# Attention's ScalarE and VectorE work issued behind the latest tanh and multiplication, in a fused attention and two-layer feed-forward kernel on one core

## The chip, the cores and the metric

The kernel runs on one core of a Trainium2 chip. The metric is device time in microseconds (us) of one execution. A core has TensorE (PE in the profile, with weight loads as PEld), VectorE (DVE), ScalarE (ACT), GpSimd (POOL) and SyncE (SP, which here issues nearly all DMAs). Each engine works through its own instructions in the order in which they stand; semaphores make one engine wait for another.

## The reference

Three parts follow each other, all in float32. Attention has 4 batches of 8 heads, 576 positions and 64 channels; it is computed twice, once on means of four neighbouring positions (144 x 144 scores) and once locally, in a band of 7 positions, and the two outputs are added. The result, 2304 tokens by 512 channels, goes through two feed-forward layers with 2048 hidden channels.

```python
out_up = np.repeat(sm_attn(q_d, k_d, v_d), factor, axis=2)      # q_d, k_d, v_d: means of 4 positions
scores = np.where(np.abs(pos[:, None] - pos[None, :]) < factor, scale * q @ k.T, -1e9)
x = out_up + softmax(scores) @ v                                 # (2304, 512) after a transpose
h = x @ w_in;  x = (h * (1 / (1 + np.exp(-1.702 * h)))) @ w_out  # layer 1
h = x @ w_in2; out = np.where(h > 0, h, np.exp(np.minimum(h, 0)) - 1) @ w_out2   # layer 2
```

## The kernel before

Every float32 operand of the layers is split into a high and a low part that TensorE multiplies at full rate (type float32r); a product is the sum of three of four partial products (high x high, high x low, low x high). ScalarE makes the high part by a copy, VectorE the low part by a subtraction.

**Units of attention.** `Unit(b, hp, ...)` is one batch and one pair of heads. Its work is cut into pieces (`pieces`, L608): `trans` or `turn` (turns q and k; batches 2 and 3 do it on VectorE), `qk` (local scores, tiles `qk`, then `sl` and row maxima `nm` on VectorE), `qk_down` (scores of the means, `qkd`, `nmd`), `exps` (exponentials on ScalarE into `sl` and `pd`, with their sums), `weigh` (division by the sums on VectorE), `pdt` and `pt` (transposes on TensorE into PSUM tiles `pdt` and `ptr`, copied to `pdT` and `PT`), `pv_down` and `pv` (products with v; the result goes to the layer's input `x32`, "x" in the rows). The PSUM tiles of all pieces share a pool `spool` of two buffers (tag `s`) once the first phase is over. A list `queue` holds the pieces of all units in order; `attend()` (L718) takes the next one, and one deferred group of three exponentials.

**Layer 1.** Tokens are in blocks (`BLOCKS1`: 256, 256, 512, 512, 512, 256). A step is one block and one inner tile (two tiles of 128 hidden channels for a block of 256 tokens, one for 512): `products_h1` (L746) multiplies x by w_in into PSUM tile `h` (two buffers), then ScalarE's tanh writes `g` (L767), VectorE multiplies (L770), ScalarE copies the high part `g1h` (L771) and VectorE subtracts the low part `g1l` (L772). `products_y1` (L780) multiplies these by w_out two steps later (`LAG`) into `y`; after the last tile of a block, `ye` goes to DRAM (`ydram`). `ye` and `g` share the two buffers of tag `g`. Steps 0 to 15 are those of blocks 0 and 1, in alternation from step 4 on (step 12 is tile 4 of block 1, step 15 its tile 7); steps 16 to 31 are block 2, 32 to 47 block 3, 48 to 63 block 4, 64 to 71 block 5.

**What sets the order.** The loop at L985 walks the steps. A step's products are generators that yield between parts, and at each yield the loop calls `attend()` once (L1016). Before a block's first step, `split_some` splits its x into `xh` and `xl` (L299, L300). A planner then orders each engine's instructions by priority and modelled readiness and keeps dependences; `tc.issue_after(ins)` adds the order (no wait) that what is traced inside the block stands behind `ins` on the engine of `ins`. It is used in layer 2 already, in `behind` (L257).

Of the kernel before, what the change touches and what calls it, by code (L numbers as in the profile page):

```python
# [15 lines left out]
AF = mybir.ActivationFunctionType  # L16
ALU = mybir.AluOpType
# [10 lines left out]
NK = 4  # L28
# [28 lines left out]

NEXTRA = 6
AHEAD = 3


def win_start(w):
# [4 lines left out]
def kernel(  # L67
# [20 lines left out]
    nc = tc.nc  # L88
# [18 lines left out]
    for half in range(2):  # L107
        rows = slice(64 * half, 64 * half + 64)
        for a, e, lo in ((0, 1, -3), (1, 5, 0), (5, 6, 3)):
            m = mask[rows, a:e, :]  # L110
            for step, base, mult in ((1, -lo, -1), (-1, lo + 6, 1)):
                nc.gpsimd.affine_select(
                    out=m, in_=m, pattern=[[0, e - a], [step, KW]], compare_op=ALU.is_ge, fill=NEG,
# [133 lines left out]
    def w_in(layer, f, c, part):  # L247
        return wts[layer, "i", f][:, part, c, :]
# [7 lines left out]
    @contextmanager  # L256
    def behind():  # L257
        with ExitStack() as stack:
            for ins in urgent.values():
                stack.enter_context(tc.issue_after(ins.ins))  # L260
            yield
# [24 lines left out]
    def block_of(gw):  # L286

        return next(i for i, (t0, n) in enumerate(BLOCKS1) if t0 <= 64 * gw < t0 + n)

    def split_x(blk, c):  # L290
        if blk not in xsplit:

            n = BLOCKS1[blk][1]
            nb = 2 if blk == 0 else 1
            parts = [xpool.tile([P, nb, NK, n], F32R, tag=f"x{p}", name=f"x{p}_{blk}") for p in "hl"]
            for i in range(nb):
                xsplit[blk + i] = [t[:, i] for t in parts]
        hi, lo = xsplit[blk]
        nc.scalar.activation(out=hi[:, c, :], in_=x32[blk][:, c, :], func=AF.Copy)  # L299
        nc.vector.tensor_tensor(  # L300
            out=lo[:, c, :], in0=x32[blk][:, c, :], in1=hi[:, c, :].bitcast(F32), op=ALU.subtract
        )
# [385 lines left out]
    for i, u in enumerate(units + [None]):  # L688
        front, nback = pieces[u] if u is not None else ([], [])
# [25 lines left out]
    def ready(blk):  # L715
        return not due[blk]

    def attend():  # L718

        if deferred:  # L720
            deferred.pop(0)()
        if not queue:
            return False
        piece, ends = queue[0]
        if ends is not None and block_of(ends.b * NWIN + ends.w1 - 1) >= nsplit[0] // NK + XBUFS:
            return False
        queue.pop(0)
        piece()
        if ends is not None:
            for users in due.values():  # L730
                users.discard(ends)
        return True

    def split_some(blk):

        if blk < NBLK and nsplit[0] < NK * (blk + 1) and ready(blk):
            split_x(blk, nsplit[0] % NK)
            nsplit[0] += 1

    hg = {}  # L740

    def tiles_of(blk):

        return 512 // BLOCKS1[blk][1]

    def products_h1(blk, st):  # L746

        xh, xl = xsplit[blk]
        nf, tb = tiles_of(blk), BLOCKS1[blk][1]
        ph = hpool.tile([P, nf, tb], F32, tag="h", name=f"h1_{blk}_{st}")  # L750
        done = 0
        for i in range(nf):
            f = nf * st + i
            n = 0
            for wp, xp in ((0, xh), (0, xl), (1, xh)):
                for c in range(NK):
                    nc.tensor.matmul(  # L757
                        out=ph[:, i, :], lhsT=w_in(1, f, c, wp), rhs=xp[:, c, :],
                        start=(n == 0), stop=(n == 3 * NK - 1),
                    )  # L760
                    n += 1
                    done += 1
                    if done == 6 * nf:
                        yield
        g = gpool.tile([P, nf, tb], F32, tag="g", name=f"g1_{blk}_{st}", bufs=2)

        nc.scalar.activation(out=g, in_=ph, func=AF.Tanh, scale=0.851)  # L767
        gh = gpool.tile([P, nf, tb], F32R, tag="gh", name=f"g1h_{blk}_{st}")
        gl = gpool.tile([P, nf, tb], F32R, tag="gl", name=f"g1l_{blk}_{st}")
        nc.vector.scalar_tensor_tensor(out=g, in0=g, scalar=1.0, in1=ph, op0=ALU.add, op1=ALU.mult)  # L770
        ins = nc.scalar.activation(out=gh, in_=g, func=AF.Copy)  # L771
        copied = nc.vector.tensor_tensor(out=gl, in0=g, in1=gh.bitcast(F32), op=ALU.subtract)  # L772
        if blk == NBLK - 1:
            urgent.update(act=ins, dve=copied)
        hg[blk, st] = (gh, gl)
        yield
# [106 lines left out]
    def split_y(bi, c):  # L883
        t0, n = blocks[bi]
        if bi not in x2:
            pool = x2pools[bi % 2]
            x2[bi] = [pool.tile([P, NK, 512], F32R, tag=f"x2{p}", name=f"x2{p}_{bi}") for p in "hl"]
        hi, lo = x2[bi]
        t = y32.pop((bi, c))
        nc.scalar.activation(out=hi[:, c, :n], in_=t[:, :n], func=AF.Copy)  # L890
        nc.vector.tensor_tensor(  # L891
            out=lo[:, c, :n], in0=t[:, :n], in1=hi[:, c, :n].bitcast(F32), op=ALU.subtract
        )
# [32 lines left out]
    def hidden2(s):  # L926
# [3 lines left out]
        if bi + 1 < len(blocks):  # L930
            if 8 <= f < 8 + NK:
                load_y(bi + 1, f - 8)
            if 10 <= f < 10 + NK:
                split_y(bi + 1, f - 10)
        wt2.load(AHEAD + wt2.half - wt2.loaded)
        with behind():
# [42 lines left out]
    def rate(si):  # L979
        if due[1] and si < 8:  # L980
            return RATE0
        return RATE1

    waiting, prev = [], None
    for si, (blk, f2) in enumerate(steps + [(None, None)] * LAG):  # L985
        chunks = []
        if blk is not None:
            while not ready(blk):
                assert attend()
            if blk > 1 and f2 == 0:  # L990

                for _ in range(NK):
                    split_some(blk)
                while waiting:
                    prev = waiting.pop(0)
                    wt1.need("o", tiles_of(prev[0]) * (prev[1] + 1) - 1)
                    chunks.append(products_y1(*prev))
            while nsplit[0] < NK * (blk + 1):
                split_some(blk)
            wt1.need("i", tiles_of(blk) * (f2 + 1) - 1)  # L1000
            chunks.append(products_h1(blk, f2))
            waiting.append((blk, f2))
            if blk == NBLK - 1:
                used |= {f"wi{2 * f2}", f"wi{2 * f2 + 1}"}
        if len(waiting) > LAG or blk is None:
            prev = waiting.pop(0)
            wt1.need("o", tiles_of(prev[0]) * (prev[1] + 1) - 1)
            chunks.append(products_y1(*prev))
        if blk is None:
            hidden2(si - len(steps))  # L1010
        nchunk = 0
        for chunk in chunks:
            for _ in chunk:
                if not wt1.finished() and blk == 0:
                    wt1.convert()
                for _ in range(rate(si)):  # L1016
                    attend()
                if blk == 0:
                    split_some(1)
                nchunk += 1  # L1020
                if wt2 is not None and nchunk in (2, 3) and (nchunk == 2 or si % 2):
                    wt2.load(AHEAD + wt2.half - wt2.loaded)
                    with behind():
                        wt2.convert()
        if blk == NBLK - 1:
            if 1 <= f2 <= NK:
                load_y(0, f2 - 1)
            if 3 <= f2 < 3 + NK:
                split_y(0, f2 - 3)
        if chunks and prev is not None and prev[0] == NBLK - 1:  # L1030
            used |= {f"wo{2 * prev[1]}", f"wo{2 * prev[1] + 1}"}
        if wt1.finished() and stage1 is not None:
            ls1.close()
            stage1 = None
        if not queue and nsplit[0] == NK * NBLK and l1a is not None:
            l1a.close()
            l1x.close()
            l1s.close()
            hpools.append(ls2.enter_context(tc.tile_pool(name="hpool2", bufs=2, space=PSUM, side="right")))
            l1a = None  # L1040
            stage2 = ls2.enter_context(tc.tile_pool(name="stage2", bufs=1, side="right"))
            x2pools.append(ls2.enter_context(tc.tile_pool(name="x2a", bufs=1, side="right")))
            wextra = ls2.enter_context(tc.tile_pool(name="wextra", bufs=1, side="right"))
            for i, tile2 in enumerate(order2):
                places[(2, *tile2)] = (wextra, f"we{i}") if i < NEXTRA else (wpool, released[i - NEXTRA])
            used |= {f"we{i}" for i in range(NEXTRA)}
            wt2 = Weights(2, order2, stage2, 3, lambda tag: tag in used, 0)
            wt2.load(AHEAD)
    assert not queue
# [46 lines left out]
```

## Time and profile before

| | |
|---|---|
| runs of the kernel before, us | 991.32, 990.57, 985.33 (median 990.57) |
| profiled execution, its own time, us | 992.29 |
| its span from first to last instruction, us | 990.5 |
| mean granted TensorE clock | 0.983 |
| TensorE busy, share of the span | 97% |
| VectorE and ScalarE busy | 50% and 47% |

A busy time counts the instructions that run, also when they run slowly: TensorE's granted clock stands beside it, in shares of full speed. Two levels occur, 2.4 GHz (1.0) and 1.2 GHz (0.5). In the rows an instruction's end is modelled, so that pipelined instructions overlap: the pace of a run of matmuls is read from one start to the next. A wait is written as [idle before <- what ended it].

### The profile page before, as it was taken

To read this page: it belongs to the slowest core of one execution; us is meant where nothing else is said; L and a number is where in the kernel's file an instruction comes from. 1 tells how busy PE (TensorE), PEld (TensorE's weight loads), DVE (VectorE), ACT (ScalarE), POOL (GpSimd) and SP (SyncE) were. 2 spreads that over 40 slices of the span, in tenths; PEclk is the share of its full clock that TensorE was granted. 3 is DMA by queue.
4 is the path that set the end of the run, shared out by engine and by line. 5 is a ranking of instruction groups with operands and counts; after the bars stand their busy time and mean duration, and the time that the engine had idled before them with its cause. 6 is when DMAs were issued, how large, how long until landed. Compare 5 with 4: busy or idle time off the path is not lost. (4 is left out here: it accounts for less than half of the span.)

```text
span 990.5 us, 15177 instructions
## 1 busy us (share of the span) xinstructions
PE 957.7 (97%) x6028; PEld 789.3 (80%) x6028; DVE 499.6 (50%) x898; ACT 468.5 (47%) x1116; POOL 69.9 (7%) x117
## 2 busy tenths in 40 slices
PE   7988999998999999999999989999999999999998
PEld 4557888976777877888888987877888888888897
DVE  2888898655555453232223898785223222322232
ACT  4899976444344362223224565665334333433343
POOL 4330034112011010000000000000000000000000
PEclk9989999988999999999999999999999999999999
DMA  9756823423222010301004960002001100100010
GB/s 188 218 159 179 251 50 55 90 44 77 50 51 61 25 52 16 126 1 43 1 1 135 357 219 11 1 1 86 1 0 32 43 1 1 54 0 1 1 43 22
DMA packets 113846, 68.01 MB, mean 69 GB/s; under 512 B 80752, under 2 KB 103792, under 8 KB 113776
## 3 DMA queue, kind: packets, MB, share of 16 engines
q1 hardware_dynamic: 109040, 65.87, 23.5%
q10 hardware_dynamic: 4736, 1.18, 0.7%
q8 instruction: 47, 0.77, 0.3%
q14 instruction: 23, 0.19, 0.1%
HBM read 57.59 MB, written 9.44 MB: 68 GB/s over the span
## 5 line engine op out<-in xcount | busy, mean ns | idle before, releaser
L792 PE MATMUL y<-g1h,whl1o 128*128 128x256 f32 (+1 forms) x768 | 208.5, 344 | 0.0
L954 PE MATMUL o<-whl2o,g2h 128*128 128x512 f32 x576 | 181.4, 395 | 3.7 <-ACT ye L801 3.4
L757 PE MATMUL h<-xh,whl1i 128*128 128x256 f32 (+1 forms) x768 | 171.5, 346 | 3.7 <-ACT xh L299 2.7
L905 PE MATMUL h<-x2h,whl2i 128*128 128x512 f32 (+1 forms) x640 | 158.9, 370 | 0.0
L792 PEld LDWEIGHTS y<-g1h,whl1o 128*128 128x128 f32 x768 | 135.8, 191 | 17.2 <-issue 1.0
L757 PEld LDWEIGHTS h<-xh,whl1i 128*128 128x128 f32 x768 | 124.2, 191 | 22.3 <-ACT xh L299 3.5
L915 DVE SCALAR_TENSOR_TENSOR g<-e,h 128x512 f32<-128x512 f32 (+1 forms) x80 | 50.7, 633 | 180.0 <-ACT e L913 179.8
L905 PEld LDWEIGHTS h<-x2h,whl2i 128*128 128x128 f32 x640 | 114.3, 188 | 22.5
L954 PEld LDWEIGHTS o<-whl2o,g2h 128*128 128x128 f32 x576 | 107.5, 189 | 28.6 <-ACT ye L801 3.8
L792 PE MATMUL y<-g1l,whl1o 128*128 128x256 f32 (+1 forms) x384 | 129.9, 339 | 0.0
L912 ACT ACTIVATE e<-h 128x512 f32<-128x512 f32 (+1 forms) x80 | 44.3, 554 | 161.6 <-PE h L905 161.6
L954 PE MATMUL o<-whl2o,g2l 128*128 128x512 f32 x288 | 113.1, 393 | 0.0
L770 DVE SCALAR_TENSOR_TENSOR g<-g,h 128x512 f32<-128x512 f32 x72 | 49.2, 684 | 121.2 <-ACT g L767 121.2
L767 ACT ACTIVATE g<-h 128x512 f32<-128x512 f32 x72 | 42.8, 595 | 134.2 <-PE h L757 128.0
L757 PE MATMUL h<-xl,whl1i 128*128 128x256 f32 (+1 forms) x384 | 88.1, 344 | 0.0
L905 PE MATMUL h<-x2l,whl2i 128*128 128x512 f32 (+1 forms) x320 | 79.6, 370 | 0.0
L792 PEld LDWEIGHTS y<-g1l,whl1o 128*128 128x128 f32 x384 | 73.6, 192 | 6.9
L922 DVE TENSOR_TENSOR g2l<-g,g2h 128x512 fp32r<-128x512 f32 (+1 forms) x80 | 51.7, 646 | 36.8 <-ACT g2h L920 21.6
L757 PEld LDWEIGHTS h<-xl,whl1i 128*128 128x128 f32 x384 | 62.5, 192 | 8.1 <-issue 0.4
L920 ACT ACTIVATE g2h<-g 128x512 fp32r<-128x512 f32 (+1 forms) x80 | 47.2, 589 | 42.9 <-DVE g L915 42.7
L905 PEld LDWEIGHTS h<-x2l,whl2i 128*128 128x128 f32 x320 | 56.7, 188 | 11.0
L771 ACT ACTIVATE g1h<-g 128x512 fp32r<-128x512 f32 x72 | 45.5, 632 | 40.3 <-DVE g L770 40.1
(109 smaller groups left out, 1152.7 us busy)
## 6 DMA issues: line engine op xcount, KB each, us to landing
wst1i<-in_moe_w_in_dram SPq DMA_DIRECT2D x16, 512.0 KB
wst1o<-in_moe_w_out_dram SPq DMA_DIRECT2D x16, 512.0 KB
wst2i<-in_moe_w_in_dram SPq DMA_DIRECT2D x16, 512.0 KB
wst2o<-in_moe_w_out_dram SPq DMA_DIRECT2D x16, 512.0 KB
vr<-in_v_dram SPq DMA_DIRECT2D x32, 144.0 KB
ydram<-ye SPq DMA_DIRECT2D x18, 256.0 KB
out_dram<-ot SPq DMA_DIRECT2D x18, 256.0 KB
y<-ydram SPq DMA_DIRECT2D x16, 256.0 KB
```

Of the source, the lines that this page charges most:

```text
L757: nc.tensor.matmul(out=ph[:, i, :], lhsT=w_in(1, f, c, wp), rhs=xp[:, c, :], start=(n == 0), stop=(n == 3 * NK - 1),)
L767: nc.scalar.activation(out=g, in_=ph, func=AF.Tanh, scale=0.851)
L770: nc.vector.scalar_tensor_tensor(out=g, in0=g, scalar=1.0, in1=ph, op0=ALU.add, op1=ALU.mult)
L771: ins = nc.scalar.activation(out=gh, in_=g, func=AF.Copy)
L792: nc.tensor.matmul(out=yps[blk][m // nf][:, m % nf, :], lhsT=w_out(1, f, wp)[:, m, :], rhs=gp[:, i, :], start=(st == 0 and n == 0 and m % ...
L905: nc.tensor.matmul(out=ph[:, :n], lhsT=w_in(2, f, c, wp), rhs=xp[:, c, :n], start=(i == 0), stop=(i == 3 * NK - 1),)
L912: nc.scalar.activation(out=e[:, :n], in_=ph[:, :n], func=AF.Relu, scale=-1.0)
L915: urgent["dve"] = nc.vector.scalar_tensor_tensor(out=g[:, :n], in0=e[:, :n], scalar=-1.0, in1=ph[:, :n], op0=ALU.add, op1=ALU.max)
L920: nc.scalar.activation(out=gh[:, :n], in_=g[:, :n], func=AF.Copy)
L922: return lambda: nc.vector.tensor_tensor(out=gl[:, :n], in0=g[:, :n], in1=gh[:, :n].bitcast(F32), op=ALU.subtract)
L954: nc.tensor.matmul(out=ops[bi][i], lhsT=gp[:, i * P:(i + 1) * P], rhs=wo[wp], start=(f == 0 and m == 0), stop=(f == NF - 1 and m == 2),)
```

## The change

`products_h1` notes its tanh and its multiplication in `evacuated`. From step 12 on, what `attend()` and the block's `split_some` issue on ScalarE is ordered behind the latest noted tanh, and what they issue on VectorE behind the latest noted multiplication. TensorE, GpSimd and SyncE get no such order. No instruction is added, dropped or resized.

```diff
+WRITTEN = 12
...
     hg = {}
+    evacuated = []
+
+    @contextmanager
+    def behind_step(si):
+        with ExitStack() as stack:
+            if si >= WRITTEN:
+                for ins in evacuated:
+                    stack.enter_context(tc.issue_after(ins.ins))
+            yield
...
-        nc.scalar.activation(out=g, in_=ph, func=AF.Tanh, scale=0.851)
+        front = nc.scalar.activation(out=g, in_=ph, func=AF.Tanh, scale=0.851)
...
-        nc.vector.scalar_tensor_tensor(out=g, in0=g, scalar=1.0, in1=ph, op0=ALU.add, op1=ALU.mult)
+        middle = nc.vector.scalar_tensor_tensor(out=g, in0=g, scalar=1.0, in1=ph, op0=ALU.add, op1=ALU.mult)
+        evacuated[:] = [front, middle]
...
-                for _ in range(NK):
-                    split_some(blk)
+                with behind_step(si):
+                    for _ in range(NK):
+                        split_some(blk)
...
-                for _ in range(rate(si)):
-                    attend()
+                with behind_step(si):
+                    for _ in range(rate(si)):
+                        attend()
```

In the rows of the order below, a number before the last number of a name is the tile or unit (`h_1_7` is block 1, tile 7; `g1h_6` is tile 6; `pd_0_0`, `sl_0_0` belong to the unit whose `pdt_2_0` and `ptr_2_0` read them, batch 2, pair 0). Line numbers of the change are higher by 2 to 12.

TensorE, steps 14 to 16, before: from the last product `y` of tile 5 of block 1 on.

```order
L792 MATMUL y_1_1813<-g1h_5_2660,whl1o_1951 128x256
L551 MATMUL pdt_2_0_0_3003<-ident,pd_0_0_2632 72x72 x4
L551 MATMUL pdt_2_0_0_3028<-ident,pd_0_0_2632 72x72 x4
L563 MATMUL ptr_2_0_0_3050<-ident,sl_0_0_2592 70x128 x4
L563 MATMUL ptr_2_0_0_3071<-ident,sl_0_0_2592 70x128 x4
L563 MATMUL ptr_2_0_0_3084<-ident,sl_0_0_2592 70x128
L573 MATMUL pvd_0_0_3100<-pdT_0_0_3002,vd_0_0_2527 64x144 x3
L757 MATMUL h_2_0_3077<-xh_2977,whl1i_815 128x512 x3
L792 MATMUL y_1_1812<-g1h_6_2773,whl1o_2173 128x256
```

The same engine in the change, from the same product on, and around the transposes of the unit.

```order
L804 MATMUL y_1_1813<-g1h_5_2660,whl1o_1951 128x256
L575 MATMUL pvd_3_0_2811<-pdT_3_0_2704,vd_3_0_2091 64x144 x4
L591 MATMUL pv_1_3_0_2829<-PT_3_0_2752,vw_3_0_2573 64x64 x10
L591 MATMUL pv_1_3_0_2854<-PT_3_0_2752,vw_3_0_2573 64x64 x8
L804 MATMUL y_1_1812<-g1h_6_2773,whl1o_2173 128x256
...
L553 MATMUL pdt_2_0_0_3003<-ident,pd_0_0_2632 72x72 x4
L804 MATMUL y_1_1813<-g1h_7_2886,whl1o_2407 128x256
...
L553 MATMUL pdt_2_0_0_3028<-ident,pd_0_0_2632 72x72 x4
L565 MATMUL ptr_2_0_0_3050<-ident,sl_0_0_2592 70x128 x4
L804 MATMUL y_1_1813<-g1l_7_2887,whl1o_2435 128x256
```

The transposes of unit (2, 0) stood in one piece ahead of the products `y` of tiles 6 and 7; they now stand among the products of tile 7, and the products of tile 6 come before them. The same happens one unit later: `pdt_2_1` and `ptr_2_1` stood in one piece behind `qkd_2_2`, ahead of `h_2_2`, and now stand among `y` of tile 0, `h_2_3` and `y` of tile 1 of block 2. From `pv_2_1` on TensorE's rows are the same but for two places in block 3, where a transpose stands one matmul earlier and another three later.

VectorE, steps 15 to 16, before: the multiplications of tiles 6 and 7 (`g_1_6`, `g_1_7`).

```order
L494 TENSOR_SCALAR nmd_1_0_2929<-nmd_1_0_2929 72x4
L300 TENSOR_TENSOR xl_2978<-x_2_932,xh_2977 128x512 x3
L435 STREAM_TRANSPOSE kT_2_0_2961<-rawk_2_0_2681 128x576
L533 TENSOR_SCALAR sumset<-sumset 128x13
L565 COPY PT_0_0_3049<-ptr_2_0_0_3050 70x512
L770 SCALAR_TENSOR_TENSOR g_1_6_2771<-g_1_6_2771,h_1_6_2739 128x512
L425 TENSOR_REDUCE kd_2_0_2965<-kT_2_0_2961 128x144
L770 SCALAR_TENSOR_TENSOR g_1_7_2884<-g_1_7_2884,h_1_7_2841 128x512
```

The same engine in the change, around the same multiplications and around those of tiles 0 and 1 of block 2.

```order
L781 SCALAR_TENSOR_TENSOR g_1_6_2771<-g_1_6_2771,h_1_6_2739 128x512
L567 COPY PT_3_0_2752<-ptr_1_3_0_2796 70x128
L781 SCALAR_TENSOR_TENSOR g_1_7_2884<-g_1_7_2884,h_1_7_2841 128x512
L784 TENSOR_TENSOR g1l_6_2774<-g_1_6_2771,g1h_6_2773 128x512
L302 TENSOR_TENSOR xl_2978<-x_2_932,xh_2977 128x512
L784 TENSOR_TENSOR g1l_7_2887<-g_1_7_2884,g1h_7_2886 128x512
L602 TENSOR_TENSOR x_2_932<-pv_1_3_0_2829,dn_3_0_2816 128x320
...
L781 SCALAR_TENSOR_TENSOR g_2_1_3162<-g_2_1_3162,h_2_1_3130 128x512
L784 TENSOR_TENSOR g1l_0_3096<-g_2_0_3093,g1h_0_3095 128x512
L602 TENSOR_TENSOR x_3_1758<-pv_2_0_0_3137,dn_0_0_3105 128x64
L602 TENSOR_TENSOR x_4_3147<-pv_2_0_0_3137,dn_0_0_3105 128x192
```

The two multiplications stood behind the scores, splits and first copy of later units, and now stand ahead of them; in exchange the additions into `x`, which free the PSUM tiles `pv`, now stand behind a multiplication and a low part.

ScalarE, steps 13 to 14, in the change; before, the nine exponentials of `sl_0_0` stood ahead of tile 5's tanh (`g_1_5`), and tile 6's tanh stood fifteen rows behind that, also behind the splits and exponentials of the next unit.

```order
L778 ACTIVATE g_1_5_2658<-h_1_5_2618 128x512
L511 ACTIVATE sl_0_0_2592,sumset<-sl_0_0_2592,nm_0_0_2593 128x70 x3
L783 ACTIVATE g1h_5_2660<-g_1_5_2658 128x512
L813 ACTIVATE ye_0_2698<-y_0_1250 128x512
...
L813 ACTIVATE ye_0_2723<-y_0_1251 128x512
...
L558 ACTIVATE pdT_3_0_2704<-pdt_1_3_0_2733 72x288
L778 ACTIVATE g_1_6_2771<-h_1_6_2739 128x512
L569 ACTIVATE PT_3_0_2752<-ptr_1_3_0_2778 70x512
```

Tile 6's tanh now follows the two `ye` of block 0 closely, whose buffers tiles 6 and 7 take over.

## Rows read from the trace of the kernel before

**Rows 1.** The page: busy us, share of the span and instructions by engine.

```profile
PE 957.7 (97%) x6028; PEld 789.3 (80%) x6028; DVE 499.6 (50%) x898; ACT 468.5 (47%) x1116; POOL 69.9 (7%) x117
```

**Rows 2.** Windows: length, busy us (count) by engine, PEclk, DMA, GB/s.

```profile
210.00:220.00 10.00, 9.18 (x45) 7.23 (x46) 6.93 (x13) 4.23 (x13) 0.00 (x0) 0.66 0.23 38
...
230.00:240.00 10.00, 6.37 (x67) 4.43 (x68) 6.46 (x15) 6.35 (x30) 2.27 (x6) 0.83 0.36 75
240.00:250.00 10.00, 10.00 (x41) 7.85 (x39) 5.50 (x10) 3.16 (x6) 2.40 (x3) 0.83 0.24 46
```

**Rows 3.** Waits of PE from 200 to 400 us: total us, times, longest.

```profile
PE pdt L551 <- ACT pd L516: 4.1, 4, 2.5
PE pvd L573 <- ACT PT L567: 0.9, 2, 0.5
```

**Rows 4.** Timeline of PE, first stall: start, us, instruction, count.

```profile
209.91 0.44 PE L551 MATMUL pdt<-ident,pd 72*72 72x72 f32 x4 [1.06 <-ACT pd L516]
...
214.16 1.65 PE L757 MATMUL h<-xh,whl1i 128*128 128x512 f32 x3
```

**Rows 5.** Timeline of PE, second stall.

```profile
235.66 0.44 PE L551 MATMUL pdt<-ident,pd 72*72 72x72 f32 x4 [2.48 <-ACT pd L516]
...
240.71 2.08 PE L757 MATMUL h<-xh,whl1i 128*128 128x512 f32 x4
```

**Rows 6.** Windows of three stretches between the same pieces of successive units.

```profile
198.53:253.11 54.58, 49.07 (x387) 39.58 (x386) 27.67 (x56) 22.61 (x79) 7.86 (x15) 0.87 0.26 55
253.11:272.58 19.47, 19.47 (x159) 15.01 (x158) 11.44 (x25) 8.22 (x33) 1.48 (x3) 1.00 0.33 63
272.58:292.55 19.97, 19.97 (x166) 15.52 (x165) 12.76 (x26) 9.62 (x36) 2.74 (x6) 1.00 0.31 62
```

**Rows 7.** The first stretch again, line 757 alone, then line 792 alone.

```profile
198.53:253.11 54.58, 18.78 (x72) 13.38 (x72) 0.87 0.26 55
...
198.53:253.11 54.58, 16.29 (x97) 14.76 (x96) 0.87 0.26 55
```

**Rows 8.** Timeline of PE: the pace of matmuls, and pieces of attention.

```profile
221.07 0.40 PE L792 MATMUL y<-g1h,whl1o 128*128 128x256 f32 x2
...
222.51 0.40 PE L792 MATMUL y<-g1h,whl1o 128*128 128x256 f32 x2
...
227.89 0.69 PE L589 MATMUL pv<-PT,vw 70*64 70x64 f32 x16
...
247.58 1.07 PE L757 MATMUL h<-xh,whl1i 128*128 128x512 f32 x4
...
250.30 0.39 PE L792 MATMUL y<-g1h,whl1o 128*128 128x512 f32 x1
...
272.58 0.71 PE L573 MATMUL pvd<-pdT,vd 72*64 72x144 f32 x8
```

**Rows 9.** Timeline of ACT: the chain behind a product h, and dn.

```profile
225.82 0.29 ACT L578 ACTIVATE dn<-pvd 128x144 f32<-128x144 f32 x1 [0.95 <-PE pvd L573]
...
250.56 0.60 ACT L767 ACTIVATE g<-h 128x512 f32<-128x512 f32 x1 [3.54 <-PE h L757]
251.91 0.63 ACT L771 ACTIVATE g1h<-g 128x512 fp32r<-128x512 f32 x1 [0.75 <-DVE g L770]
```

**Rows 10.** Timeline of DVE: the additions into x, and a multiplication.

```profile
228.65 0.49 DVE L600 TENSOR_TENSOR x<-pv,dn 128x64 f32<-128x64 f32 x2 [1.68 <-PE pv L589]
...
251.19 0.69 DVE L770 SCALAR_TENSOR_TENSOR g<-g,h 128x512 f32<-128x512 f32 x1 [3.44 <-ACT g L767]
```

**Rows 11.** Timeline of SP's queue: start, us, DMA issues.

```profile
191.03 1.94 SPq L355 DMA_DIRECT2D rawk<-in_k_dram  x4
193.07 0.96 SPq L802 DMA_DIRECT2D ydram<-ye  x2
```

**Rows 12.** The chain of waits, layer 1's end: start, us, what.

```profile
535.97 2.92 DMA ydram<-ye
539.62 4.33 DMA ydram<-ye
```

## The prediction

> **What bounds the kernel now.** The page comes first [rows 1]: TensorE is busy 97% of the span, VectorE and ScalarE about half of it. So a change of order on VectorE and ScalarE can gain only where TensorE waits for them, or where it runs slowly because it has waited. The windows of 10 us say where that is in the steps that the change touches [rows 2]: from 210 to 220 and from 230 to 250 us the granted clock is 0.66, 0.83 and 0.83, and in the window from 230 TensorE is busy only 6.37 of 10 us. The list of TensorE's waits from 200 to 400 us [rows 3] has only two entries that matter, `pdt` behind the exponentials of `pd` (4.1 us in 4 waits) and `pvd` behind the copy `PT` (0.9 us in 2). The timeline shows both places: at 209.91 us the transposes `pdt` of one unit have waited 1.06 us [rows 4], at 235.66 us those of the next have waited 2.48 us [rows 5]. Behind each, the clock has fallen to its lower level, 1.2 GHz: four 512-column matmuls from 240.71 us on take 2.08 us [rows 5], where at 247.58 us they take 1.07 us [rows 8].
>
> Both places are what the order left there: the work of a whole unit, exponentials to transposes, stands on TensorE in one piece with no product beside it, because the products `y` of tiles 6 and 7 and `h_2_2` are behind multiplications that VectorE does late.
>
> **The size of the loss.** I take the stretch from `pvd_1_3` to `pv_2_1`, 198.53 to 253.11 us, which holds the same TensorE instructions in both orders (the change only has one tile of 24 products ahead of `pvd_1_3` instead of behind it). It lasts 54.58 us at a mean clock of 0.87, with TensorE busy 49.07 us, so 5.5 us idle [rows 6]. What would the same work take undisturbed?
> - Its products are 72 of line 757 and 97 of line 792 by the rows [rows 7], 96 of them in program order (one began before the stretch). 96 of the 168 have 256 columns, 72 have 512. Twelve of 256 columns take 1.44 us (221.07 to 222.51) and twelve of 512 take 2.72 us (247.58 to 250.30) [rows 8]: 11.5 + 16.3 = 27.8 us.
> - Attention in it is two whole units and one more `pvd`. The undisturbed period from one `pvd` to the next is 19.97 us, at a clock of 1.00 [rows 6], with five tiles of twelve 512-column products, 13.6 us. That leaves 6.4 us for a unit, switches between the shapes included. Two units and one `pvd` (0.7 us, [rows 8]) are 13.5 us.
>
> Together 41.3 us, against 54.58: the stretch loses 13.3 us. Of these 5.5 are idle, about 7.1 are clock (0.13 of 54.58), and the rest lies in short transposes whose modelled ends hide small waits.
>
> **What the change moves, and what it costs.** Nothing is added, so no engine gets more work; the waits are what can change. Tiles 6 and 7 are multiplied before the scores of the next unit, so their 48 products (5.8 us) and then block 2's first tiles stand between the pieces of attention. While exponentials, division and transposition of a unit run on ScalarE and VectorE, TensorE now has products. The two waits for `pd` lose their cause. In their place come these:
> - `qk_2_1` needs a PSUM buffer that the addition of `pv_1_3` into x frees. On VectorE this addition is now behind the low part of tile 7, which is behind `g1h` on ScalarE, behind `dn`, behind `pvd`. From `pvd` to the free buffer: 0.29 + 0.63 [rows 9], 0.69 for the low part at the multiplication's size, and 0.49 for the addition [rows 10], 2.1 us. TensorE has two groups of `pv` (0.7 us each, [rows 8]) and two products meanwhile, 1.6 us: 0.5 us open.
> - `qk_2_2`'s second half needs the buffer of `pv_2_0`, whose additions are behind the multiplication of tile 1 and the low part of tile 0. From the end of `h_2_1`: tanh 0.60 [rows 9], multiplication and low part 0.69 each, additions 0.49 [rows 10], about 2.5 us. TensorE has `pv` 0.7, half a `qk` as long, and one product: 1.6 us. Open: 0.9 us.
> - ScalarE does 9 exponentials of `sl_2_1` and 4 of `pd_2_1` ahead of `pdT_2_0`, and the transposes of unit (2, 0) wait for its buffers. No row shows this wait; it lies between nothing and the 1.06 us of the first stall [rows 4]. I take 0.5.
> - The exponentials of `sl_2_0` now stand ahead of `pdT_1_3`, which releases a buffer for `ptr_1_3`: between 0 and 1.06 us by the same bounds; I take 0.4.
> - Tile 6's tanh takes a buffer of `ye`, so it waits until `ye` has landed in DRAM, and ScalarE's queue waits behind it. SP issues `ye` after `rawk` at 193.07 us [rows 11]; `rawk` waits for a transpose that now stands behind tile 5's tanh and multiplication, later by some 1.3 us (0.60 + 0.69, [rows 9, 10]). Landings took 2.92 and 4.33 us [rows 12], so the buffer is free about 200 us. Nobody on TensorE needs `g1h_6` before the 48 products of tile 7's `h` and tile 5's `y` (5.8 us from about 199) and the pieces `pvd` and `pv` (2 us) are done. Cost: nothing, as long as the landing takes under about 8 us.
> - GpSimd and SP get their work in nearly the same order; loads of q, k, v are issued units ahead. Nothing.
>
> New waits: 0.5 + 0.9 + 0.5 + 0.4 = 2.3 us, at best 1.4 (the last two at zero), at worst 5.5 (as much idle time as the stretch has now). If the clock stays up, the gain is 13.3 - 2.3 = **11.0 us**, between 7.8 and 11.9. Behind the stretch TensorE's rows are the same, and everything up to the end follows TensorE, so the gain should reach the end whole. The profiled execution (992.29 us) would become 981.3; it is 1.7 us over the median of the runs, and from the median (990.57) I forecast **979.5 us**. By its own bounds the forecast's range is 978.5 to 983.
>
> **The rivals.**
> 1. *One clock fall stays.* The clock fell after TensorE had done little but waits and small transposes [rows 4, 5]. The new waits are short, but that of `qk_2_2` falls among small matmuls. A fall costs about half of the 7.1 us, 3.5: 983.0 us. For: 0.9 us of waiting near short pieces. Against: in the two periods behind the stretch the same short pieces stand among products and the clock is 1.00 [rows 6]. Chance 0.20; that both falls stay (986.5 us), 0.08.
> 2. *The gain is given back later.* At layer 1's end there is a chain over `ydram` with 2.92 and 4.33 us of DMA [rows 12]. If that stretch were set by something that doesn't come earlier with TensorE, the time would be 990.6. Against: its `ye`, reloads and weight loads are all released by TensorE's own progress. Chance 0.05.
> 3. *Slower: the waits for PSUM buffers bring the clock down in every unit.* If the additions into x stand behind a multiplication in each of the eight units of batches 2 and 3, TensorE may fall to 1.2 GHz once in each, at 3.5 us: 979.5 + 28 = 1007.5 us. It decides from four units on (14 us, more than the gain). Against it: from `pv_2_1` on the order hardly changes, and those units run at 1.00 now [rows 6]. Chance 0.03. The Trainium skill speaks for this rival: TensorE: Matmul & The Clock Gate, in "A second HAM failure mode: psum-queue depth-cycling", tells of a kernel whose TensorE idled briefly and often between groups of matmuls as it cycled through PSUM buffers, and whose clock went up and down for it. By that rule the clock's share of the loss would stay even with the long waits gone; the rows of the two later periods, which cycle through the same two buffers at 1.00, don't bear it out here.
>
> That the change does nothing is excluded by the order of the rows; that it gains more than the whole loss of 13.3 us (under 977.3) I see no row for.
>
> **How the numbers follow.** Forecast 0.64, rival 1 0.28 in its two forms, rival 2 0.05, rival 3 0.03. The forecast's case and one remaining fall hold 0.84. With about 2 us for the scatter of the medians, since the runs of before lie between 985.33 and 991.32, the range is 976 to 985.5. 1% is 9.9 us, about what a measurement of this kernel can tell from no change: the line is at 980.7. The forecast's case lies under it in about eight of ten outcomes (the new waits have to stay under 3.4 us), 0.51, and rival 1 hardly: faster 0.52. Slower is rival 3, 0.03; within 1% the rest, 0.45.
>
> **What would show it.** Right: no wait of `pdt` for `pd` over 1 us; PEclk of 1.00 in every window from 200 to 260 us; 41 to 46 us from the end of the last `y` of tile 4 to `pv_2_1`, against about 54; short waits of `qk` for VectorE's x at two places; a DMA wait on ScalarE before tile 6's tanh that nobody feels. Wrong: a clock under 1.00 in those windows, `h_2_0` waiting for `xl`, `pv_1_3` waiting for `PT`, or a stretch from 530 to 600 us that has grown by what the first one lost.

## The result, and the profile after

The change takes 980.93 us (median of 6 runs, 979.55 to 983.48) against 990.91 us for the kernel before (6 runs, 985.33 to 992.43). The ratio of the means (981.02 and 989.74 us) is 0.9912, with a 95% interval of [0.9888, 0.9936]: a gain of 8.7 us, between 6.3 and 11.1. The medians differ by 10.0 us. The forecast was 979.5 us, in a range from 976 to 985.5. The profiled execution of the change took 983.48 us, with a span of 981.7 us and a mean granted clock of 0.986.

The page's engine line (busy us, share of the span, instructions) has the same instructions as [rows 1], and 4.5 us less of TensorE's busy time:

```profile
PE 953.2 (97%) x6028; PEld 787.2 (80%) x6028; DVE 500.2 (51%) x898; ACT 467.7 (48%) x1116; POOL 69.0 (7%) x117
```

Of TensorE's waits from 200 to 400 us (total us, times, longest), which in [rows 3] were 4.1 us for `pd` and 0.9 us for `PT`, one line is left, and it is another one:

```profile
PE qk L461 <- DVE x L602: 1.3, 2, 0.7
```

The timeline of TensorE (start, us, instruction, count, and in brackets the wait before it) shows both places. The `pdt` of the first one, which had waited 1.06 us [rows 4], starts at 217.25 us with no wait, its second half at 218.02; that of the second one, which had waited 2.48 us [rows 5], at 235.39 us. Before each stand products `y`, and after each come products or further transposes. The two new waits are those of `qk`, 0.58 and 0.75 us. Four 512-column matmuls of `h` take 1.20 us at 224.31, not the 2.08 us of [rows 5].

```profile
210.04 0.83 PE L461 MATMUL qk<-kT,qT 64*64 64x70 f32 x20 [0.58 <-DVE x L602]
...
217.13 0.28 PE L804 MATMUL y<-g1h,whl1o 128*128 128x256 f32 x1
217.25 0.41 PE L553 MATMUL pdt<-ident,pd 72*72 72x72 f32 x4
217.46 0.36 PE L804 MATMUL y<-g1h,whl1o 128*128 128x256 f32 x1
...
218.02 0.41 PE L553 MATMUL pdt<-ident,pd 72*72 72x72 f32 x4
...
224.31 1.20 PE L768 MATMUL h<-xh,whl1i 128*128 128x512 f32 x4
...
229.89 0.71 PE L461 MATMUL qk<-kT,qT 64*64 64x70 f32 x16 [0.75 <-DVE x L602]
...
235.15 0.40 PE L804 MATMUL y<-g1h,whl1o 128*128 128x512 f32 x1
235.39 0.41 PE L553 MATMUL pdt<-ident,pd 72*72 72x72 f32 x4
235.60 0.48 PE L804 MATMUL y<-g1h,whl1o 128*128 128x512 f32 x1
```

VectorE's timeline says why `qk` waits: the additions into x at 209.51 and 229.26 us, which free the buffer, stand directly behind a low part `g1l`, as the working had it.

```profile
208.84 0.74 DVE L784 TENSOR_TENSOR g1l<-g,g1h 128x512 fp32r<-128x512 f32 x1 [1.79 <-ACT g1h L783]
209.51 0.48 DVE L602 TENSOR_TENSOR x<-pv,dn 128x320 f32<-128x320 f32 x1
...
228.66 0.68 DVE L784 TENSOR_TENSOR g1l<-g,g1h 128x512 fp32r<-128x512 f32 x1
229.26 0.48 DVE L602 TENSOR_TENSOR x<-pv,dn 128x64 f32<-128x64 f32 x2
```

The windows of 10 us (length, busy us and counts by engine, PEclk, DMA share, GB/s) that answer to [rows 2] had 0.66, 0.83 and 0.83; the granted clock is now 1.00, that is 2.4 GHz, in each:

```profile
210.00:220.00 10.00, 9.96 (x106) 9.16 (x107) 9.73 (x21) 6.58 (x31) 1.36 (x3) 1.00 0.61 122
...
230.00:240.00 10.00, 10.00 (x69) 7.86 (x69) 7.08 (x16) 6.17 (x30) 1.37 (x3) 1.00 0.34 72
240.00:250.00 10.00, 10.00 (x108) 7.73 (x108) 4.78 (x11) 2.60 (x5) 2.57 (x6) 1.00 0.35 69
```

Now the whole span in three parts: up to the stretch of [rows 6], the stretch, and all behind it. First the two outer parts of the kernel before:

```profile
0.00:198.53 198.53, 179.60 (x1732) 146.62 (x1733) 153.87 (x309) 147.56 (x420) 49.63 (x75) 0.96 0.58 149
253.11:990.50 737.39, 729.08 (x3911) 603.14 (x3910) 318.10 (x534) 298.30 (x617) 12.42 (x27) 1.00 0.16 48
```

Then the three parts of the change:

```profile
0.00:201.40 201.40, 182.69 (x1733) 148.79 (x1734) 154.43 (x308) 147.08 (x419) 48.50 (x75) 0.94 0.58 145
201.40:244.54 43.14, 41.81 (x389) 35.26 (x389) 27.71 (x57) 22.66 (x79) 5.79 (x12) 1.00 0.35 78
244.54:981.70 737.16, 728.74 (x3914) 603.13 (x3910) 318.04 (x533) 297.97 (x618) 14.74 (x30) 1.00 0.15 48
```

The stretch went from 54.58 to 43.14 us, 11.4 us less, and all behind it stayed (737.39 and 737.16). But the first part is 2.9 us longer, at a clock of 0.94 instead of 0.96, so that the two profiled spans differ by 8.8 us only. TensorE's instructions there are the same in the same order, and ScalarE's and VectorE's are up to 185 us of the kernel before; the sections below come back to it.

### The profile page after: what moved, and what is told of

It reads as the page before. It is cut to its first block, busy times and chain, and to the rows that moved or that the text cites. A ratio compares the mean times of both kernels' runs of the same rounds, so it can differ in the third digit from the quotient of the medians.

```text
span 981.7 us, 15180 instructions
## 1 busy us (share of the span) xinstructions
PE 953.2 (97%) x6028; PEld 787.2 (80%) x6028; DVE 500.2 (51%) x898; ACT 467.7 (48%) x1116; POOL 69.0 (7%) x117
## 5 line engine op out<-in xcount | busy, mean ns | idle before, releaser
L768 PE MATMUL h<-xh,whl1i 128*128 128x256 f32 (+1 forms) x768 | 169.4, 343 | 3.7 <-ACT xh L301 2.5
L966 PEld LDWEIGHTS o<-whl2o,g2l 128*128 128x128 f32 x288 | 54.4, 189 | 12.0
```

What stands on the lines that cost most here:

```text
L768: nc.tensor.matmul(out=ph[:, i, :], lhsT=w_in(1, f, c, wp), rhs=xp[:, c, :], start=(n == 0), stop=(n == 3 * NK - 1),)
L966: nc.tensor.matmul(out=ops[bi][i], lhsT=gp[:, i * P:(i + 1) * P], rhs=wo[wp], start=(f == 0 and m == 0), stop=(f == NF - 1 and m == 2),)
```

## The experiments

My theory: the gain is the two stalls of `pdt` and the clock falls behind them, and nothing else; what removes them is that the multiplications of tiles 6 and 7 (first stall) and of tiles 0 and 1 (second stall) come before the next units' work. The rivals: the new order gains in many small places, up to layer 1's end; only one of the two engines' orders matters; a short PSUM wait would cost a clock fall as well.

**The change from step 20 only.** 990.35 us, ratio to the kernel before 0.9995 [0.9972, 1.0019].

```diff
-WRITTEN = 12
+WRITTEN = 20
```

> The order of the change from step 20 on only. Theory 1 (the whole gain lies in the one stretch from the end of tile 4's y to pv_2_1, steps 12 to 18): no gain, ratio to before 0.998 to 1.002, both waits of pdt (about 1.1 and 2.5 us) and both falls of the clock are back, the stretch is about 54.6 us. Rival (every unit of batches 2 and 3 gains a little, about 1.25 us each): five of eight units keep their gain, ratio about 0.994.

The waits of TensorE from 200 to 400 us are back to what [rows 3] shows:

```profile
PE pdt L553 <- ACT pd L518: 3.7, 3, 2.4
PE pvd L575 <- ACT PT L569: 0.9, 2, 0.5
PE qkd L488 <- DVE sl L472: 0.2, 1, 0.2
```

The order on 52 of the 60 steps that the change touches gives no gain that these runs can tell. The first part and the stretch:

```profile
0.00:198.81 198.81, 180.26 (x1732) 147.50 (x1733) 154.51 (x309) 147.76 (x420) 49.11 (x75) 0.96 0.59 148
198.81:251.13 52.32, 47.20 (x388) 38.02 (x387) 27.55 (x56) 22.70 (x79) 7.88 (x15) 0.90 0.27 57
```

With both waits, this stretch takes 52.32 us at a clock of 0.90, where [rows 6] has 54.58 at 0.87. Idle time hardly differs (52.32 - 47.20 = 5.12 us against 5.51), so most of the 2.3 us is clock. The expectation that both falls of the clock come back was wrong: behind the first wait, as long as that of [rows 4], the clock stays at 1.00, and behind the second it is low for longer.

```profile
210.19 0.44 PE L553 MATMUL pdt<-ident,pd 72*72 72x72 f32 x4 [1.05 <-ACT pd L518]
```

```profile
210.00:220.00 10.00, 8.99 (x67) 7.62 (x68) 7.21 (x14) 4.51 (x15) 0.00 (x0) 1.00 0.26 42
...
230.00:240.00 10.00, 7.09 (x34) 4.71 (x33) 6.39 (x15) 7.52 (x32) 1.35 (x3) 0.60 0.46 82
240.00:250.00 10.00, 10.00 (x41) 8.17 (x40) 4.44 (x7) 2.16 (x5) 2.45 (x3) 0.89 0.04 14
```

**Steps 14 to 16 only.** 980.81 us, ratio 0.9883 [0.9857, 0.991]: the whole gain from three of 72 steps, with a ratio just under the expected range. The two `qk` waits stay (1.3 us together), the stretch takes 43.15 us.

```diff
-            if si >= WRITTEN:
+            if 14 <= si <= 16:
```

> The order of the change in steps 14 to 16 only, nothing behind them. Theory 1: the full gain, ratio to before 0.989 to 0.993, a stretch of 42 to 44 us at a clock of 1.00, with the two short waits of qk for x that the change has (0.58 and 0.75 us). Rival (every unit gains): one or two units of eight, ratio about 0.998.

**One engine's order alone.** ScalarE alone: 980.03 us, ratio 0.9885 [0.9864, 0.9906], just under the expected range. VectorE alone (`evacuated[1:]`): 983.74 us, ratio 0.9921 [0.9899, 0.9943].

```diff
-                for ins in evacuated:
+                for ins in evacuated[:1]:
```

> Only ScalarE's half of the order: attention and splits behind the latest tanh, VectorE free. If the exponentials ahead of the tanh make the loss, this keeps the gain: ratio 0.989 to 0.993; only one of the two short waits of qk is left, at qk_2_2. If the late multiplications on VectorE make it: ratio about 0.998 to 1.000 and a stretch of 52 us or more.

> Only VectorE's half: behind the latest multiplication, ScalarE free. A multiplication cannot run before its tanh, so if the two halves pull each other along, this also keeps most of the gain: ratio 0.990 to 0.995, with somewhat longer waits for VectorE at qk_2_1 and qkd_2_2 (2 to 3 us in all against 1.3). If the exponentials on ScalarE make the loss alone: ratio about 1.000.

Either half alone takes both stalls away. Their stretches, ScalarE's order first, are both at a clock of 1.00:

```profile
201.22:243.44 42.22, 41.47 (x387) 34.86 (x388) 26.93 (x55) 21.47 (x77) 6.16 (x12) 1.00 0.33 71
```

```profile
199.82:244.16 44.34, 42.26 (x388) 35.18 (x388) 27.44 (x57) 22.28 (x78) 5.47 (x12) 1.00 0.35 77
```

They differ in the new waits, in the kernel with ScalarE's order one of 0.8 us:

```profile
PE qk L461 <- DVE x L602: 0.8, 1, 0.8
```

and with VectorE's three, of 2.0 us together:

```profile
PE qk L461 <- DVE x L602: 1.0, 1, 1.0
PE qkd L488 <- DVE sl L472: 1.0, 2, 0.8
```

With ScalarE's order alone, the first addition into x stands ahead of `g1l` of tile 7, not behind it, and the wait of 0.58 us at `qk_2_1` is gone. So the first new wait belongs to VectorE's half. That half adds no gain to ScalarE's: with both, the stretch is 0.9 us longer (43.14 against 42.22), which is too little to see in the medians.

**From step 16 on.** 984.50 us, ratio 0.9943 [0.9918, 0.9968].

```diff
-WRITTEN = 12
+WRITTEN = 16
```

> The order of the change from step 16 on. Steps 12 to 15 are as before, and the order begins with block 2. Theory 1 (two stalls, one at each end of the stretch, each with its wait and its fall of the clock): the first stall stays in part, with waits of 1 to 3 us at pdt_2_0 and behind it, the second goes; about half of the gain, ratio 0.993 to 0.996, stretch 46 to 50 us. Rival (one cause for both: once tiles 6 and 7 are late, the rest follows): nearly no gain, ratio over 0.997.

The first stall stays, the second goes:

```profile
212.75 0.44 PE L553 MATMUL pdt<-ident,pd 72*72 72x72 f32 x4 [0.93 <-ACT pd L518]
214.96 1.22 PE L768 MATMUL h<-xh,whl1i 128*128 128x512 f32 x2 [1.04 <-ACT xh L301]
```

```profile
201.50:248.94 47.44, 44.46 (x388) 37.49 (x389) 27.91 (x56) 21.84 (x78) 5.45 (x12) 0.93 0.29 63
```

The stretch stands 4.3 us over the change's 43.14, and the median 3.6 us over 980.93: that is one stall, waits and fall together. Its clock share, (1 - 0.93) x 47.44 = 3.3 us, is close to the 3.5 us that rival 1 put on a fall; idle time is 2.98 us against 1.33. The two overlap where TensorE waits at the lower clock.

**Only the splits behind the tanh and the multiplication** (`attend()` as before): 990.19 us, ratio 1.0004 [0.9976, 1.0032].

```diff
-                with behind_step(si):
-                    for _ in range(rate(si)):
-                        attend()
+                for _ in range(rate(si)):
+                    attend()
```

> Only the splits of x at a block's first step stand behind the tanh and the multiplication, attend's pieces do not. Theory 1 (attention's pieces hold back the multiplications): no gain, ratio 0.998 to 1.002 and both waits of pdt as before. Rival (the four splits, 2.2 us of ScalarE and 2.5 us of VectorE, hold them back): a gain of 4 us or more, ratio 0.996 or less.

Both stalls are back (`pdt` waits 0.93 and 2.21 us, and `ptr` and `h` wait 0.7 us each behind the first). The first part is the shortest of all these kernels:

```profile
0.00:195.45 195.45, 177.85 (x1732) 145.57 (x1732) 154.12 (x309) 147.56 (x420) 47.32 (x75) 0.97 0.60 151
195.45:248.44 52.99, 47.34 (x387) 38.60 (x388) 28.07 (x56) 22.24 (x78) 5.46 (x12) 0.90 0.27 57
```

Where the multiplications of the four tiles stand on VectorE (number of the instruction in the order of its trace) sorts all these kernels:

```
kernel            tile 6  tile 7   tile 0  tile 1   stalls
before               329     331      355     356   both
from step 20         329     331      355     356   both
splits only          327     328      354     355   both
from step 16         324     325      338     340   the first
steps 14 to 16       309     311      338     340   none
ScalarE's alone      310     311      338     340   none
VectorE's alone      309     312      338     343   none
the change           309     311      338     340   none
```

The stall is there where the tile's multiplication stands late, whichever engine's order put it there.

**One wait by itself, short and long.** Far from the stretch, in layer 2, the relu of one inner tile is written 20 times, then 26 times, over the same values (one run each, 981.76 and 985.43 us; the change itself scatters by 4 us, so only the rows count here).

```diff
-        nc.scalar.activation(out=e[:, :n], in_=ph[:, :n], func=AF.Relu, scale=-1.0)
+        for _ in range(20 if s == 40 else 1):
+            nc.scalar.activation(out=e[:, :n], in_=ph[:, :n], func=AF.Relu, scale=-1.0)
```

> The change, and in layer 2 the relu of tile 40 issued 20 times over the same data instead of once, some 10 us more on ScalarE at one place, with nothing else changed. TensorE has the tiles it is ahead by (about 8 us), so it should wait about 1 to 2 us once. Theory 1 (short waits among whole tiles of products leave the clock up): the granted clock stays 1.00 and the place costs its wait alone. Rival (any wait of over 1 us brings a fall): a stretch at 1.2 GHz of 3 to 7 us behind it, costing 1.5 to 3.5 us more.

> The same with 26 relus, some 3 us more on ScalarE: TensorE should wait about 5 us once. Theory 1 (a long wait brings the clock down, and the fall is a cost of its own): the granted clock is 0.5 for 3 to 10 us behind the wait, and the same products take longer by half of that, 1.7 to 5 us on top of the wait. Rival (the clock costs nothing, since other engines are behind anyway after a wait): the place costs its wait alone, within 0.5 us.

With 20, TensorE's timeline and the window around it:

```profile
810.41 0.97 PE L917 MATMUL h<-x2h,whl2i 128*128 128x512 f32 x3 [0.85 <-DVE g L928]
```

```profile
810.00:820.00 10.00, 9.59 (x42) 7.72 (x43) 4.92 (x8) 5.37 (x10) 0.00 (x0) 1.00 0.00 0
```

The wait of 0.85 us leaves the clock at 1.00. It came out shorter than the expected 1 to 2 us, so this run does not test the rival's wait of over 1 us. Other runs bear on that: the clock stayed up behind 1.05 us (from step 20), and fell behind 1.06 us (before) and 0.93 us (from step 16, and splits only, there with further waits of 0.7 to 1.0 us close behind), all of them at the same `pdt`. So the length of the wait alone does not decide. With 26, the same matmul waits 4.60 us, and the clock falls during the wait:

```profile
812.04 0.79 PE L917 MATMUL h<-x2h,whl2i 128*128 128x512 f32 x1 [4.60 <-DVE g L928]
...
816.27 0.39 PE L967 MATMUL o<-whl2o,g2l 128*128 128x512 f32 x1
```

```profile
805.00:810.00 5.00, 2.44 (x11) 1.63 (x9) 0.00 (x0) 4.75 (x8) 0.00 (x0) 0.94 0.00 0
810.00:815.00 5.00, 2.96 (x6) 2.08 (x7) 3.27 (x5) 4.17 (x8) 0.00 (x0) 0.50 0.00 0
```

From 812.04 to 816.27 us nine matmuls start; they took 4.23 us, and at the full pace (2.72 us for twelve, [rows 8]) would take 2.04. The fall cost 2.2 us on top of the wait, half of the time at 1.2 GHz in which TensorE had products; the rest of that time lay in the wait.

**Fewer pieces at a time.** ScalarE's order alone, and two calls of `attend()` at a yield where there were three (this changes the order of earlier steps too): 979.57 us (975.99 to 982.45), ratio 0.9897 [0.9868, 0.9927]. Both new `qk` waits are gone, one of 0.47 us (`pvd` for `PT`) takes their place. The ratio lies in the second of the two expected ranges, but its interval reaches into the first, and the time cannot be told from the change's. In its profile the first 196.5 us have a clock of 0.99, but that is the fastest of its six runs, so it stays open whether its order has fewer falls there.

```diff
-RATE0 = 3
+RATE0 = 2
...
-                for ins in evacuated:
+                for ins in evacuated[:1]:
```

> ScalarE's half of the order (as in the run of that alone), and in steps 0 to 7 two pieces of attention at a yield instead of three (RATE0 2), to see whether the same kind of loss can be taken from the stage ahead of step 12, where TensorE waits 1 to 2 us at pdt, h and ptr and the clock is at its lower level for some 17 to 24 us in every profile. If fewer pieces at a time leave more products between them: shorter waits there, ratio to before 0.983 to 0.988. If that stage is bound by VectorE and ScalarE as a whole: the pieces left over come later, in steps 8 to 16, and the ratio is 0.988 to 0.995.

## Why the prediction was right

**The place and the mechanism: right.** Both `pdt` waits went, with both clock falls; without steps 12 to 19 no gain can be told (from step 20: 0.9995), with 14 to 16 alone all of it is there (0.9883). TensorE has products beside the exponentials because tiles 6 and 7 (0 and 1 of block 2 in the second place) are multiplied early.

One thing the working leaves unsaid is what the two waits were for. `pdt_2_0` reads the `pd` of its own unit, which was divided on VectorE at 192.88 us, 17 us before. But its two halves start at 209.91 and 210.63 us, when ScalarE has just done the second and the fourth exponential of `pd_2_1`. These read the next unit's `qkd_2_1`, which stands ahead of `pdt_2_0` on TensorE and takes both buffers of `spool`:

```profile
209.66 0.20 ACT L516 ACTIVATION_READ_ACCUMULATOR pd<-qkd,nmd 72x1 f32 x1
...
210.37 0.20 ACT L516 ACTIVATION_READ_ACCUMULATOR pd<-qkd,nmd 72x1 f32 x1
```

The second stall is alike (second exponential of `pd_2_2` done at 235.60 us, `pdt_2_1` at 235.66). So both were waits for PSUM buffers, and in the change this cause is still there: the second exponential is done at 216.5 us. TensorE only comes to `pdt` later, at 217.25 us, because it has the products of tile 7 first.

**The undisturbed stretch: right.** Worked out as 41.3 us plus 2.3 us of new waits, 43.6; measured 43.14, and 43.15 to 43.18 in the three other profiles with this order there (steps 14 to 16, 20 and 26 relus). TensorE is idle for 43.14 - 41.81 = 1.33 us of it, which is the two `qk` waits, and the rest is 0.5 us over the sum of products and pieces.

**The new waits, one by one.** `qk_2_1`: 0.5 taken, 0.58 measured. `qk_2_2`: 0.9 taken, 0.75 measured. `pdT_2_0` behind the exponentials (0.5) and `ptr_1_3` behind `pdT_1_3` (0.4): both zero, the lower end of their bounds, which makes their sum 1.33 us and not 2.3. In ScalarE's timeline the last exponentials of `pd` are done at 217.2 us, and the two halves of `pdt` start at 217.25 and 218.02 us, each directly behind a product:

```profile
216.76 0.37 ACT L518 ACTIVATE pd<-qkd,nmd 72x144 f32<-72x144 f32 x1
217.02 0.20 ACT L518 ACTIVATION_READ_ACCUMULATOR pd<-qkd,nmd 72x1 f32 x1
217.76 0.41 ACT L558 ACTIVATE pdT<-pdt 72x288 f32<-72x288 f32 x1 [0.54 <-PE pdt L553]
```

**The landing that nobody feels: right, with its size off.** ScalarE's tanh of tile 6 waits 4.38 us for `ye` to land, until 202.19 us where I had put about 200:

```profile
202.19 0.60 ACT L778 ACTIVATE g<-h 128x512 f32<-128x512 f32 x1 [4.38 <-DMA ydram<-ye]
```

TensorE is in products of `h` then (201.40 to 204.28 us) and goes on with `y`, with no wait before that of `qk`, which ends at 210.04 us.

**The size of the loss: somewhat too large.** The 13.3 us came from one profiled execution, 7.1 of them clock. The same two stalls cost 54.58 us there, 52.32 and 52.99 us in the profiles of two kernels that kept them, with a clock share of 7.1, 5.2 and 5.3 us ((1 - PEclk) times the stretch). Their mean, 53.3, less 43.14 is 10.2 us, against 11.0 in the forecast. The medians differ by 10.0 us, so that 979.5 became 980.93. This is the step of the sum that was mis-sized: how long the lower clock lasts behind the same wait, and whether it falls at all, is not the same in each execution. Behind the first wait the clock share was 3.4 us in the kernel before, (1 - 0.66) x 10 us, and nothing in the kernel from step 20. So the forecast's closeness of 1.4 us is in part luck: one profile could have given a loss some 2 us smaller. I had put 0.52 on a gain of over 1%; the ratio of 0.9912 lies just short of it, and its interval holds both sides.

**The part ahead of the stretch: not in the working.** I took it as the same, since its order is. It lasted 195.45, 198.53, 198.81 and 201.40 us in four kernels, at a clock of 0.97, 0.96, 0.96 and 0.94: (1 - PEclk) times its length is 5.9, 7.9, 8.0 and 12.1 us, so its clock explains the spread of 6 us but for about 1.5 us. The runs of the kernel before went from 982.85 to 994.75 us in all, with mean clocks of 0.993 and 0.977 in runs near those ends; I had put 2 us on the scatter of the medians. A single pair of profiles would have told 8.8 us where the stretch alone tells 11.4.

The change does not make these early falls. In the change they all lie in the first 120 us, and the first ScalarE or VectorE instruction that stands elsewhere than before starts after 180 us:

```profile
0.00:120.00 120.00, 103.92 (x916) 74.23 (x917) 85.39 (x176) 97.94 (x273) 26.54 (x57) 0.90 0.75 192
120.00:201.40 81.40, 78.76 (x819) 74.55 (x818) 69.04 (x133) 49.15 (x147) 21.96 (x18) 1.00 0.33 75
```

The two kernels with the relus, which have the change's order up to layer 2, take 198.16 and 196.61 us for this part, and the one from step 16, which has the old order there, 201.50 us.

**The rivals.** One fall left (rival 1): no, every window from 200 to 260 us is at 1.00; its price of 3.5 us fits the clock share of 3.3 us in the kernel from step 16. Gain given back later (rival 2): no, 737.16 us against 737.39. PSUM waits that bring the clock down in every unit (rival 3): no; the Trainium skill's rule (TensorE: Matmul & The Clock Gate, "A second HAM failure mode: psum-queue depth-cycling") is about idles that are brief and many. Here waits of 0.58, 0.75 and, by itself, 0.85 us left the clock at 1.00, and `qk` waits in two places only, so no run shows the case of that rule. The clock did fall with the wait of 4.60 us; and the two stalls of the kernel before, few and longer, were waits for PSUM buffers as well.

## What to carry to other kernels

Where an engine that looks 97% busy waits at two places, cost those places by themselves: idle time, plus half of the time at the lower clock in which it has work. In this kernel TensorE's next products hung on ScalarE's and VectorE's work on the newest one; putting work for later units behind it in three of 72 steps was enough. Take the size of a clock loss from several profiles, since the same two waits were followed by 5.2 to 7.1 us of it, and the first alone by anything from nothing to 3.4.

## What the runs showed that I had not expected

- ScalarE's order alone and VectorE's alone each take both stalls away (42.22 and 44.34 us for the stretch): the multiplication needs its tanh, and the next units' exponentials need their scores, so holding either engine holds the other. That this is how one half moves the other is argued from the dependences and not shown; the table of numbers shows that the multiplications move in both.
- The part before the stretch, with the same TensorE instructions in the same order, varies by 6 us between the profiled executions of these kernels (195.45 to 201.50), in step with the clock.
- The clock fell inside one wait of 4.60 us, not after it (0.50 in the whole window from 810 to 815 us, of which TensorE waited 2.04), so a part of the slow time cost nothing.
